# The opening of a fused attention and expert kernel: first pair head by head, its row of maxima placed by transposes, second pair's loads on ScalarE's queue

## The chip, the cores and the metric

The kernel runs on one core of a Trainium2 chip, as one launch. The metric is the device time of that launch in microseconds (us). Five engines matter here: TensorE (PE in the profile, its weight loads PEld), VectorE (DVE), ScalarE (ACT), GpSimd (POOL) and SyncE (SP), whose queue issues nearly all DMAs. Data live in SBUF (128 partitions); TensorE writes PSUM.

## The reference

Two stages, cut to what matters:

```python
# attention: q, k, v are (8, 8, 1152, 64) float32
q_pool = q.reshape(B, H, S // 2, 2, D).mean(axis=3)          # 576 queries a head
scores = scale * np.matmul(q_pool, k.transpose(0, 1, 3, 2))
scores = scores - np.max(scores, axis=-1, keepdims=True)
attn = np.exp(scores)
attn = attn / (np.sum(attn, axis=-1, keepdims=True) + 1e-09)
x = np.matmul(attn, v)                                        # then to (4608, 512)
# experts: 8 of them, one for each token
logits = x @ w_gate + modality_bias[modality_id]
e_idx = np.argmax(logits, axis=1)                             # and the gate's softmax weight
out[e_idx == e] = gate_w * (np.maximum(x[e_idx == e] @ w1[e], 0) @ w2[e])
```

All of it is computed to float32's accuracy, with float16 matmuls over high and low parts.

## The kernel before, in words

**Pairs.** The 64 heads of attention are done in 32 pairs: two heads at a time, the first on partitions 0 to 63, the second on 64 to 127. For each pair the loads bring `rawq` (queries, the two to be averaged lying in the two halves of the row), `rawk` and `rawv`. The two query halves are added (`split_q`), keys and queries are copied to float16 (`hi`, `qh`, functions `split_hi` and `split_qh`), and what the copies lose is kept as `lo` (`split_lo`).

**Maxima.** The softmax needs each query's largest score. `QB` holds the 1152 queries of a pair as nine blocks of 128. Head 0's queries stand in partitions 0 to 63 and zeros below; head 1's the other way round. Block 4 is shared: 64 queries of head 0 and 64 of head 1. So one matmul of a block with the keys `hi` of both heads gives the scores of the right head for each query. VectorE reduces them to maxima `mp`. `maxpass` does a pair; for the first pair `first_max` does blocks 0 to 4 on thirds of the keys ahead of everything, and `maxpass` the last four blocks.

**Row.** `row` takes the maxima of some blocks, turns them from a column into rows by a matmul with the identity (L792), scales them into `mr` (L801) and sends `mr` by DMA (L802) into partition 64 of `B2`.

**Scores.** `scores` makes transposed scores: a matmul with `B1` (high keys twice, over high and low queries, L888), then one with `B2` (low keys and, in partition 64, the row of the maxima, L889). So the maximum is subtracted by the matmul itself. ScalarE's exponential follows (L890, four to a third of a head's keys), then the low part `Pl` (L871 on ScalarE, L873 on VectorE). `B1` and `B2` are filled by SBUF to SBUF moves on SyncE's queue (`place_k`, `place_q`, `place_lo`, L618).

**Values.** `square` and `power` find a power of two to scale a pair's values by (L729, L735, `scales`); `values` makes their high part `VH` (L772) and low part `vl` (L765, L766), `shifted` the copy `VS` (L782). `pv` multiplies exponentials and values, three matmuls for a block (L947 to L949).

**Order.** TensorE, ScalarE, VectorE and GpSimd run in the order in which the program issues. After the opening, a loop of steps runs, 18 for a pair. In each step the letters of `ORD` say what comes when: `M` and `X` advance the maxima, `s` the scores, `v` the value products, `F` what falls due. Work is put at steps by `at`, `later` and `later_end`; the constants at the top of the file are its due steps. The value products of the first pair follow their exponentials by `LAG0` = 7 steps. `busy` issues matmuls of zeros that nothing uses.

**The opening** (L1014 to L1085) prepares pair 0 for both heads at once, then pair 1, runs `first_max` in between, places pair 0, and ends with three maxima of the rest.

After attention come routing and the experts' matmuls, which the change does not touch.

Of the kernel before, what the change touches and what calls it, by code (L numbers as in the profile page):

```python
# [22 lines left out]
P = 128  # L23
# [5 lines left out]
S = 1152  # L29
# [42 lines left out]
V0 = (0, 1, (2, 3), 3, (3, 4))  # L72
# [72 lines left out]
T_PRE = 3  # L145
# [438 lines left out]
def attention(tc, ctx, att, ident, npairs, xpool, on_two, on_split, on_scale, jobs, side, set_pm, started, ahead, hip):  # L584
# [31 lines left out]

    def move(o, i):
        nc.sync.dma_start(out=o, in_=i)  # L618

    half_q = lambda i: slice(i * 288, (i + 1) * 288)  # L620

    def load_kq(p):
        k, q = (pa.tile([P, S], F32, name="raw" + x) for x in "kq")
        st[p]["k"], st[p]["q"] = k, q
        if p == 0:
            two = lambda x: x.rearrange("p (w n) -> p w n", w=2)
            for x, i in ((q, 0), (k, 0), (k, 1), (q, 1), (k, 2)):
                if x is q:
                    nc.sync.dma_start(out=two(q)[:, :, half_q(i)], in_=two(att[p, :, S:2 * S])[:, :, half_q(i)])
                else:  # L630
                    nc.sync.dma_start(out=k[:, i * 384:(i + 1) * 384], in_=att[p, :, i * 384:(i + 1) * 384])
        else:
# [65 lines left out]
    half = [slice(0, D), slice(D, P)]  # L698

# [7 lines left out]
    def place_k(p, heads):  # L707

        s = st[p]
        for i in range(2):  # L710
            for j in heads:
                move(s["B1"][half[i], kcol(j)], s["hi"][half[j]])
# [71 lines left out]
    def row(p, mp, u0, u1):  # L784
# [13 lines left out]
        def put(pt):  # L798
# [3 lines left out]
            done = (nc.sync if p or u0 else nc.scalar).dma_start(out=B2[p % 2][D:D + 1, 2 * S + u0 * P:2 * S + u1 * P], in_=mr[0:n])  # L802
# [6 lines left out]
    def maxpass(p, mp=None):  # L809

        s = st[p]
        need(p, *(("qh", "hi0", "hi1") if p else ()))
        u0 = 0 if mp is None else 5
        two = p in TWO_ROWS
        rest = []
        if mp is None:
            mp = sm.tile([P, 9, 3], F32, name="mp")
# [20 lines left out]
    def first_max(p):  # L838

        s = st[p]  # L840
        mp = s["mp"] = sm.tile([P, 9, 3], F32, name="mp")
        for i, (u, t) in enumerate([(u, t) for us in ((0, 1), (2, 3, 4)) for t in range(3) for u in us]):
            pt = ps_sc.tile([P, 512], F32, name="psc") if i % 2 else ps_max.tile([P, 512], F32, name="pm")
            nc.tensor.matmul(pt[:, 0:384], QB[p % 2][:, u], s["hi"][:, t * 384:(t + 1) * 384], start=True, stop=True)
# [3 lines left out]
        busy(8)  # L848
        row(p, mp, 0, 5)()
# [167 lines left out]
    nc.gpsimd.memset(warm, 0.0)  # L1017
    nc.scalar.activation(warm, warm, AF.Exp)
    nc.gpsimd.memset(ones, 1.0)
    load_kq(0)  # L1020
# [9 lines left out]
    busy(7)  # L1030
    for i in range(2):
        nc.vector.memset(QB[i], 0.0)
    nc.gpsimd.memset(B2[0][D:D + 1, 0:2 * S], ROW)
    split_q(0)
    q0, qb = st[0]["q"][:, 0:SQ], QB[0].rearrange("p u n -> p (u n)")
# [583 lines left out]
```

## Time and profile before

| | |
|---|---|
| Time, median of 3 runs | 1135.43 us (1134.61 to 1135.49) |
| The profiled execution's own time | 1135.75 us |
| Its span, first to last instruction | 1134.0 us |
| TensorE busy | 1105.3 us, 97% |
| VectorE busy | 979.1 us, 86% |
| ScalarE busy | 914.1 us, 81% |
| GpSimd busy | 417.2 us, 37% |
| Granted TensorE clock, mean | 0.998 |

In the views that follow, a row of the timeline has the start, the duration, the engine, the line, the operation, what it writes and reads, its shape and count, and in brackets how long the engine was idle before and what ended that. A row of the stretches has the stretch, its length, and for PE, PEld, DVE, ACT and POOL the busy time with the count of instructions started, then the granted clock, the share of DMA and the GB/s.

### The profile page before, as it was taken

How to read it: one execution, taken by the hardware profiler on the slowest of the kernel's cores; microseconds unless marked ns; L12 is line 12 of the kernel's file. 1: busy time of each engine (PE TensorE's matmuls, PEld its weight loads, DVE VectorE, ACT ScalarE, POOL GpSimd, SP SyncE). 2: the span in 40 equal slices, each digit the busy share in tenths (PEclk: the TensorE clock that was granted, in tenths of full speed). 3: DMA queues.
4: the chain of work that ended last, by engine and by line, in shares of the span. 5: the costliest groups of instructions: out<-in, count | busy, mean ns of one | idle time of the engine just before them, and what ended most of it. 6: DMA issues, size and time to landing. Idle time of an engine off the chain costs nothing. (4 is left out here: it accounts for less than half of the span.)

```text
span 1134.0 us, 36903 instructions
## 1 busy us (share of the span) xinstructions
PE 1105.3 (97%) x15117; PEld 814.7 (72%) x15117; DVE 979.1 (86%) x1968; ACT 914.1 (81%) x1462; POOL 417.2 (37%) x408
## 2 busy tenths in 40 slices
PE   8999999999999999999999999999999999999997
PEld 4777777777777777777777777767667667667665
DVE  7999999999999999999999999887996766756754
ACT  5999999999999999999999988865556665655654
POOL 7854444354444445344444342124113112122111
PEclk9999999999999999999999999999999999999999
DMA  7677867859759768678587463499999999899993
GB/s 230 183 189 175 193 162 170 196 151 202 164 161 206 163 167 190 163 174 194 146 197 187 134 138 94 140 299 269 262 290 275 279 302 283 266 282 248 307 269 107
DMA packets 175522, 232.67 MB, mean 205 GB/s; under 512 B 92303, under 2 KB 126751, under 8 KB 175344
## 3 DMA queue, kind: packets, MB, share of 16 engines
q1 hardware_dynamic: 169254, 210.45, 71.3%
q0 software_dynamic: 6080, 19.78, 6.7%
q8 instruction: 120, 1.97, 0.7%
q14 instruction: 58, 0.48, 0.1%
q10 hardware_dynamic: 10, 0.00, 0.0%
HBM read 146.11 MB, written 18.99 MB: 146 GB/s over the span
## 5 line engine op out<-in xcount | busy, mean ns | idle before, releaser
L890 ACT ACTIVATE Pe<-psc 128x432 int32<-128x432 f32 x768 | 377.4, 526 | 44.3 <-PE psc L889 35.1
L822 DVE TENSOR_REDUCE mp<-pm 128x1 f32<-128x512 f32 x566 | 372.7, 684 | 14.2 <-PE pm L821 6.9
L947 PE MATMUL xp<-VH,Pe 128*128 128x65 f16 x2880 | 372.5, 193 | 0.0
L949 PE MATMUL xp<-VS,Pl 128*128 128x65 f16 x2880 | 371.9, 193 | 0.4 <-DVE Pl L873 0.4
L948 PE MATMUL xp<-vl,Pe 128*128 128x64 f16 x2880 | 370.6, 192 | 0.0
L948 PEld LDWEIGHTS <-Pe 128*128 128x128 f16 x2880 | 267.6, 98 | 87.5
L888 PE MATMUL psc<-B 128*128 128x432 f16 (+2 forms) x1152 | 304.0, 286 | 2.4 <-ACT Pe L890 2.2
L889 PE MATMUL psc<-B 65*128 65x432 f16 (+2 forms) x1152 | 304.7, 287 | 0.2 <-DMA B<-mr 0.2
L947 PEld LDWEIGHTS <-Pe 128*128 128x128 f16 x2880 | 272.0, 98 | 45.6 <-issue 7.5
L949 PEld LDWEIGHTS <-Pl 128*128 128x128 f16 x2880 | 266.5, 97 | 0.7 <-DVE Pl L873 0.5
L871 ACT ACTIVATE Pl<-Pe 128x1152 f16<-128x1152 uint16 (+1 forms) x190 | 219.3, 1154 | 6.0
L821 PE MATMUL pm<-hi,QB 128*128 128x512 f16 x566 | 213.8, 379 | 8.4 <-DVE mp L822 8.0
L683 POOL TENSOR_TENSOR lo<-rawk,hi 128x576 f16<-128x576 f32 (+1 forms) x68 | 87.9, 1296 | 196.5 <-ACT hi L667 183.6
L770 POOL TENSOR_SCALAR VH<-rawv,sc 128x512 f16<-128x512 f32 (+1 forms) x60 | 103.3, 1732 | 153.5 <-PE xp L949 73.8
L1296 PE MATMUL ph<-xpart,w1l 128*128 128x256 f16 x544 | 148.3, 273 | 0.0
L1295 PE MATMUL ph<-xpart,w1h 128*128 128x256 f16 x544 | 148.3, 273 | 0.0
L1294 PE MATMUL ph<-xpart,w1h 128*128 128x256 f16 x544 | 148.3, 273 | 0.0
L889 PEld LDWEIGHTS <-B 65*128 65x128 f16 x1152 | 112.8, 98 | 25.9 <-issue 3.2
L888 PEld LDWEIGHTS <-B 128*128 128x128 f16 x1152 | 112.5, 98 | 9.2 <-issue 3.8
L1300 DVE SCALAR_TENSOR_TENSOR hl<-ph,hh 128x512 f16<-128x512 f32 x72 | 49.7, 690 | 77.6 <-ACT hh L1299 77.5
L1299 ACT ACTIVATE hh<-ph 128x512 f16<-128x512 f32 x72 | 43.0, 598 | 87.5 <-PE ph L1296 87.5
L1389 PE MATMUL po<-w2h,hl 128*128 128x512 f16 x288 | 109.1, 379 | 0.0
(276 smaller groups left out, 1924.4 us busy)
## 6 DMA issues: line engine op xcount, KB each, us to landing
w2r<-in_w_dram SPq DMA_DIRECT2D x76, 512.0 KB
w1r<-in_w_dram SPq DMA_DIRECT2D x72, 512.0 KB
rawv<-in_att_dram SPq DMA_DIRECT2D x32, 576.0 KB
B<-hi SPq DMA_DIRECT2D x128, 144.0 KB
rawq<-in_att_dram SPq DMA_DIRECT2D x31, 576.0 KB
rawk<-in_att_dram SPq DMA_DIRECT2D x31, 576.0 KB
B<-qh SPq DMA_DIRECT2D x128, 72.0 KB
B<-lo SPq DMA_DIRECT2D x64, 144.0 KB
```

Source lines behind the costliest of these rows:

```text
L821: nc.tensor.matmul(pm, QB[p % 2][:, u], s["hi"][:, t * 512:(t + 1) * 512], start=True, stop=True)
L822: nc.vector.tensor_reduce(mp[:, u, t:t + 1], pm, op=ALU.max, axis=AX.X)
L871: nc.scalar.activation(low, rest, AF.Copy, scale=LOW)
L888: nc.tensor.matmul(o, b1[:, ks], b1[:, qs], start=True, stop=False, skip_group_check=True)
L889: nc.tensor.matmul(o, b2[:, ks], b2[:, qs], start=False, stop=True, skip_group_check=True)
L890: nc.scalar.activation(Pe[:, D + x0:D + x1], pt, AF.Exp, scale=1.0 / 16)
L947: nc.tensor.matmul(out, Ph[:, qs], vh[:, c, j, 0:D + 1], start=c == 0 and g == 0, stop=False, skip_group_check=True)
L948: nc.tensor.matmul(out[:, 0:D], Ph[:, qs], vl[:, c, j], start=False, stop=False, skip_group_check=True)
L949: nc.tensor.matmul(out, Pl[:, qs], vs[:, c, j, 0:D + 1], start=False, stop=c == NKC - 1, skip_group_check=True)
L1294: nc.tensor.matmul(o, hi[:, c, fs], xh[:, :, c], start=c == 0, stop=False)
L1295: nc.tensor.matmul(o, hi[:, c, fs], xl[:, :, c], start=False, stop=False)
L1296: nc.tensor.matmul(o, lo[:, c, fs], xh[:, :, c], start=False, stop=c == 3)
```

## The change

The first pair's preparation is done one head after the other. Head 0's keys are copied into a tile `hz` of their own, with zeros in partitions 64 to 127; head 1's keys stay in `hi`, with zeros in partitions 0 to 63. Blocks 0 to 3 of the first maxima use `hz` alone, and block 4 is two matmuls added up, one over each tile. Loads, adds, copies, remainders and moves of the first pair are split by head.

The row of the first five blocks no longer goes through `mr` and a DMA. The maxima are reduced into the last column of `spread`, a tile of zeros 65 wide for each block, and five transposes bring that column to partition 64 of PSUM, from where VectorE (two blocks) and ScalarE (three) write it to `B2`.

The second pair's queries and keys are loaded from ScalarE's queue. Its copies (`split_q`, `split_hi`, `split_qh`) come after the row and its remainders (`split_lo`) at step 3. The first pair's square and scale are done in the opening, its values two steps earlier. Small memsets move from GpSimd to VectorE and ahead of the first add. The numbers of filler matmuls change, and two loads are issued behind a move.

```diff
+T_L1 = 3
-V0 = (0, 1, (2, 3), 3, (3, 4))
+V0 = (None, None, (0, 1), 2, (2, 5))
-T_PRE = 3
+T_PRE = 2
...
-        B2.append(const.tile([D + 1, 2 * KQ], F16, name=f"B2_{i}"))
+        B2.append(const.tile([D + 1, 2 * KQ + (0 if i else D)], F16, name=f"B2_{i}"))
...
     def move(o, i):
-        nc.sync.dma_start(out=o, in_=i)
+        moved[:] = [nc.sync.dma_start(out=o, in_=i).ins]
+    def behind(ins, fn):
+        with tc.issue_after(ins):
+            fn()
...
         if p == 0:
-            for x, i in ((q, 0), (k, 0), (k, 1), (q, 1), (k, 2)):
...
+            for i in range(2):
+                nc.scalar.dma_start(out=two(q[half[0]])[:, :, half_q(i)], in_=two(att[p, half[0], S:2 * S])[:, :, half_q(i)])
+            for i in range(3):
+                nc.sync.dma_start(out=k[half[0], third(i)], in_=att[p, half[0], third(i)])
+            nc.sync.dma_start(out=q[half[1]], in_=att[p, half[1], S:2 * S])
+            nc.sync.dma_start(out=k[half[1]], in_=att[p, half[1], 0:S])
+        elif p > 1:
...
+    def first_max(mp):
+        for i, (u, t) in enumerate([(u, t) for us in ((0, 1), (2, 3), (4,)) for t in range(3) for u in us]):
...
+            keys = (hz, st[0]["hi"])[0:1 + u // 4]
+            for h in keys:
+                nc.tensor.matmul(pt[:, 0:384], QB[0][:, u], h[:, third(t)], start=h is hz, stop=h is keys[-1])
             nc.vector.tensor_reduce(mp[:, u, t:t + 1], pt[:, 0:384], op=ALU.max, axis=AX.X)
             busy(1, 256)
             yield
-        busy(8)
-        row(p, mp, 0, 5)()
+    def first_row(mp, spread):
+        nc.vector.tensor_reduce(spread[:, :, D], mp[:, 0:5], op=ALU.max, axis=AX.X, negate=True)
+        ends(0)
+        for us in ((0, 1), (2, 3, 4)):
+            pt = some(0)
+            for i, u in enumerate(us):
+                nc.tensor.transpose(pt[0:D + 1, i * P:(i + 1) * P], spread[:, u], ident)
+            x0, x1 = us[0] * P, (us[-1] + 1) * P
+            o, x = B2[0][D:D + 1, 2 * S + x0:2 * S + x1], pt[D:D + 1, 0:x1 - x0]
+            if us[0]:
+                nc.scalar.activation(o, x, AF.Copy, scale=1.0 / ROW, bias=16.0 * math.log(PSC) / ROW)
+            else:
+                nc.vector.tensor_scalar(o, x, 1.0 / ROW, 16.0 * math.log(PSC) / ROW, op0=ALU.mult, op1=ALU.add)
+        made.add((0, "row5"))
...
-    busy(7)
+    busy(9)
...
+    spread = const.tile([P, 5, D + 1], F32, name="turned")
+    nc.gpsimd.memset(spread, 0.0)
+    hz = pa.tile([P, S], F16, name="hi")
     split_q(0)
+    for j in range(2):
+        nc.vector.memset((hz, st[0]["hi"])[j][half[1 - j]], 0.0)
+    for b in B2:
+        nc.gpsimd.memset(b[D:D + 1, 0:2 * S], ROW)
+    for i in range(3):
+        nc.vector.memset(VH[i][:, :, :, D:D + 2], 1.0)
+        nc.vector.memset(VS[i][:, :, :, D:D + 2], 2.0 ** -16)
+    for pe, pl in PT:
+        for x in (slice(0, D), slice(D + W3, 2 * D + W3)):
+            nc.vector.memset(pe[:, x].bitcast(F32), 0.0)
+            nc.vector.memset(pl[:, x], 0.0)
+    add = lambda eng, r, c: eng.tensor_tensor(q0[r, c], q0[r, c], q1[r, c], op=ALU.add)
+    add(nc.vector, half[0], half_q(0))
+    add(nc.gpsimd, half[0], half_q(1))
...
+    for i in range(3):
+        nc.scalar.copy(hz[half[0], third(i)], k0[half[0], third(i)])
+        if i < 2:
+            if npairs > 1:
+                nc.scalar.dma_start(out=st[1]["qk"[i]], in_=att[1, :, slice((1 - i) * S, (2 - i) * S)])
+            nc.scalar.copy(qb[half[0], half_q(i)], q0[half[0], half_q(i)])
         for _ in range(2):
             next(first)
...
+    few, rest = slice(0, 5 * P - SQ), slice(5 * P - SQ, SQ)
+    add(nc.vector, half[1], few)
+    for j, h in enumerate((hz, hi)):
+        if j:
+            add(nc.gpsimd, half[1], rest)
+            nc.scalar.copy(hi[half[1]], k0[half[1]])
+            nc.scalar.copy(qb[half[1], SQ:5 * P], q0[half[1], few])
+            square(0)
+            nc.scalar.copy(qb[half[1], 5 * P:S], q0[half[1], rest])
+        nc.scalar.copy(qh[half[j]], q0[half[j], every])
+        nc.gpsimd.tensor_tensor(lo[half[j], 0:S], k0[half[j]], h[half[j]], op=ALU.subtract)
+        nc.gpsimd.tensor_tensor(lo[half[j], S:KQ], q0[half[j], every], qh[half[j]], op=ALU.subtract)
+        place_k(0, (j,))
+        place_q(0, (j,))
+        place_lo(0, (j,), 1)
+        place_lo(0, (j,), 0)
+    drain(first)
+    power(0)
+    busy(4)
+    first_row(mp0, spread)
     if npairs > 1:
         split_q(1)
         for i in range(3):
             split_hi(1, i)
         split_qh(1)
-        for i in (3, 4, 5, 6, 0, 1, 2):
-            split_lo(1, i)
-    drain(first)
...
-    mxq.append(maxpass(0, mp0))
+    mxq.append(second_max(mp0))
     for _ in range(T_PRE):
-        busy(2)
+        busy(1)
         advance(mxq, 1)
-    busy(2)
-    at(T_RT, 0, started)
+    at(T_RT, 0, lambda ins=moved[0]: behind(ins, started))
...
+            for i in (3, 4, 5, 6, 0, 1, 2):
+                go(T_L1 - b, split_lo, i)
             go(T_P1 - b, place, end=False)
             go(T_M1 - b, lambda p: mxq.append(maxpass(p)), end=False)
-            go(T_LV, load_v)
+            go(T_LV, lambda p, ins=moved[0]: behind(ins, lambda: load_v(p)))
```

More of the change, by code (lines that the diff above doesn't have):

```diff
@@ L615, in need @@
         assert all((p, n) in made for n in names), f"pair {p}: {names} are not made yet"
+    moved = []
     def move(o, i):
-        nc.sync.dma_start(out=o, in_=i)
+        moved[:] = [nc.sync.dma_start(out=o, in_=i).ins]
+    def behind(ins, fn):
+        with tc.issue_after(ins):
+            fn()
     half_q = lambda i: slice(i * 288, (i + 1) * 288)
+    third = lambda i: slice(i * 384, (i + 1) * 384)
+    half = [slice(0, D), slice(D, P)]
     def load_kq(p):
@@ L711, in place_k @@
             for j in heads:
-                move(s["B1"][half[i], kcol(j)], s["hi"][half[j]])
+                move(s["B1"][half[i], kcol(j)], (s["hi"] if p or j else hz)[half[j]])
     def place_lo(p, heads, k):
@@ L847, in first_max, with second_max @@
             yield
-        busy(8)
-        row(p, mp, 0, 5)()
+    def first_row(mp, spread):
[12 more added lines that the diff above has]
+        made.add((0, "row5"))
+    def second_max(mp):
+        s = st[0]
+        for u in range(5, 9):
+            for t in range(2):
+                pm = ps_max.tile([P, 512], F32, name="pm")
+                nc.tensor.matmul(pm, QB[0][:, u], s["hi"][:, t * 512:(t + 1) * 512], start=True, stop=True)
+                nc.vector.tensor_reduce(mp[:, u, t:t + 1], pm, op=ALU.max, axis=AX.X)
+                yield
+        pm = ps_max.tile([P, 512], F32, name="pm").rearrange("p (n k) -> p n k", k=P)
+        for i in range(4):
+            nc.tensor.matmul(pm[:, i], QB[0][:, 5 + i], s["hi"][:, 1024:S], start=True, stop=True, skip_group_check=True)
+        nc.vector.tensor_reduce(mp[:, 5:9, 2], pm, op=ALU.max, axis=AX.X)
+        yield
+        later_end(FIN if now[0] > NSTEP else 1, row(0, mp, 5, 9))
     def scores(p, j, r):
@@ new lines, in attention @@
+    qb = QB[0].rearrange("p u n -> p (u n)")
+    q0, q1 = (st[0]["q"][:, i * SQ:(i + 1) * SQ] for i in range(2))
+    k0, hi, qh, lo = (st[0][x] for x in ("k", "hi", "qh", "lo"))
+    for b in B2:
[7 more added lines that the diff above has]
+            nc.vector.memset(pl[:, x], 0.0)
@@ L1036, in attention @@
+    first = first_max(mp0)
+    add = lambda eng, r, c: eng.tensor_tensor(q0[r, c], q0[r, c], q1[r, c], op=ALU.add)
+    every = slice(0, SQ)
+    add(nc.vector, half[0], half_q(0))
+    add(nc.gpsimd, half[0], half_q(1))
     if npairs > 1:
         load_kq(1)
-    first = first_max(0)
-    for n, i in ((0, 0), (2, 1), (2, 2)):
+    for i in range(3):
+        nc.scalar.copy(hz[half[0], third(i)], k0[half[0], third(i)])
         if i < 2:
-            both = st[0]["q"].rearrange("p (w n) -> p w n", w=2)
-            nc.vector.tensor_tensor(both[:, 0, half_q(i)], both[:, 0, half_q(i)], both[:, 1, half_q(i)], op=ALU.add)
-        if i == 0:
-            nc.scalar.copy(qb[0:D, half_q(0)], q0[0:D, half_q(0)])
-        split_hi(0, i)
-        if i == 1:
-            nc.scalar.copy(qb[0:D, half_q(1)], q0[0:D, half_q(1)])
+            if npairs > 1:
+                nc.scalar.dma_start(out=st[1]["qk"[i]], in_=att[1, :, slice((1 - i) * S, (2 - i) * S)])
+            nc.scalar.copy(qb[half[0], half_q(i)], q0[half[0], half_q(i)])
@@ L1108, in attention @@
             go = lambda t, f, *a, p=p: at(t, p, lambda: f(p, *a))
-        go(sq, square)
-        go(power_, power)
+        if p:
+            go(sq, square)
+            go(power_, power)
         for i, t in enumerate(vh):
```

49 lines of the change are left out of this document (8 added, 41 removed).

## The prediction

> **What bounds the kernel now.** I read the page's busy shares first, then the busy time by stretches of ten microseconds, then the opening engine by engine in order of time, because everything the change touches runs before the third pair.
>
> ```profile
> span 1134.0 us, 36903 instructions
> PE 1105.3 (97%) x15117; PEld 814.7 (72%) x15117; DVE 979.1 (86%) x1968; ACT 914.1 (81%) x1462; POOL 417.2 (37%) x408
> ...
> 10.00:20.00 10.00, 10.00 (x48) 5.31 (x47) 8.60 (x17) 2.57 (x7) 9.58 (x35) 1.00 0.82 196
> 20.00:30.00 10.00, 7.61 (x49) 3.99 (x48) 8.28 (x21) 9.90 (x17) 7.06 (x5) 1.00 0.64 220
> 30.00:40.00 10.00, 9.89 (x160) 7.34 (x160) 9.60 (x23) 9.91 (x18) 6.68 (x6) 1.00 0.96 276
> ...
> 19.40:30.20 10.80, 8.41 (x55) 4.51 (x54) 9.08 (x22) 10.64 (x18) 7.80 (x9) 1.00 0.63 211
> 30.20:49.20 19.00, 18.45 (x304) 13.98 (x303) 18.46 (x45) 18.76 (x33) 14.70 (x12) 1.00 0.70 188
> ```
>
> TensorE is busy 97% of the span and from 30 us on it hardly pauses, so the time is its remaining work plus the moment when that work can run without gaps. That moment is the first value product. From 19.4 to 30.2 us it is ScalarE that has no idle time (10.64 of 10.80), while TensorE starts only 55 instructions; from 30.2 on both are full. What the change can win is therefore the shift of the first value product, and it is worth as much at the end. The rows of the opening, ScalarE, VectorE, GpSimd, TensorE and SyncE's queue in turn:
>
> ```profile
> 4.26 0.43 ACT L1044 CAST QB<-rawq 64x288 f16<-64x288 f32 x1 [1.96 <-DVE rawq L1042]
> 4.60 0.51 ACT L667 CAST hi<-rawk 128x384 f16<-128x384 f32 x1
> 13.00 1.34 ACT L667 CAST hi<-rawk 128x384 f16<-128x384 f32 x3 [2.87 <-DMA rawk<-in_att_dram]
> 14.24 0.67 ACT L657 CAST qh<-rawq 128x576 f16<-128x576 f32 x1
> 16.76 1.28 ACTq L802 DMA_DIRECT2D B<-mr  x1
> 19.40 1.12 ACT L890 ACTIVATE Pe<-psc 128x432 int32<-128x432 f32 x2 [4.50 <-PE psc L889]
> 20.42 1.16 ACT L729 ACTIVATE vl<-rawv 128x1152 f16<-128x1152 f32 x1
> 21.57 0.52 ACT L890 ACTIVATE Pe<-psc 128x432 int32<-128x432 f32 x1
> ...
> 1.26 1.14 DVE L1032 MEMSET QB<- 128x576 uint32 x2
> 3.77 0.46 DVE L1042 TENSOR_TENSOR rawq<-rawq 128x288 f32<-128x288 f32 x1 [1.36 <-DMA rawq<-in_att_dram]
> 5.67 0.56 DVE L845 TENSOR_REDUCE mp<-pm 128x1 f32<-128x384 f32 x1 [1.45 <-PE pm L844]
> 9.42 0.56 DVE L845 TENSOR_REDUCE mp<-pm 128x1 f32<-128x384 f32 x1 [0.51 <-PE pm L844]
> 14.70 0.55 DVE L845 TENSOR_REDUCE mp<-pm 128x1 f32<-128x384 f32 x1
> 15.28 0.17 DVE L788 TENSOR_REDUCE m<-mp 128x5 f32<-128x15 f32 x1
> 16.45 0.28 DVE L801 TENSOR_SCALAR mr<-pj 5x128 f16<-5x128 f32 x1 [0.99 <-PE pj L792]
> 23.02 0.22 DVE L743 TENSOR_SCALAR sc<-half 128x1 int32<-128x1 int32 x2
> 23.15 0.14 DVE L743 TENSOR_SCALAR scales<-half 128x1 int32<-128x1 int32 x1
> ...
> 1.13 2.01 POOL L1033 MEMSET B<- 1x2304 f16 x1
> 11.82 1.40 POOL L648 TENSOR_TENSOR rawq<-rawq 128x576 f32<-128x576 f32 x1
> 13.59 2.79 POOL L683 TENSOR_TENSOR lo<-rawk,hi 128x288 f16<-128x288 f32 x4 [0.37 <-ACT hi L667]
> 16.34 1.55 POOL L683 TENSOR_TENSOR lo<-rawq,qh 128x192 f16<-128x192 f32 x3
> 17.84 0.13 POOL L1073 MEMSET VH<- 128x36 f16 x1
> 19.72 2.01 POOL L1079 MEMSET B<- 1x2304 f16 x1
> 32.82 1.29 POOL L683 TENSOR_TENSOR lo<-rawq,qh 128x576 f16<-128x576 f32 x1
> ...
> 16.14 0.27 PE L792 MATMUL pj<-ident,m 128*5 128x128 f32 x1
> 19.02 0.35 PE L889 MATMUL psc<-B 65*128 65x432 f16 x1
> 30.22 0.19 PE L947 MATMUL xp<-VH,Pe 128*128 128x65 f16 x1
> ...
> 3.76 0.43 SPq L633 DMA_DIRECT2D rawq<-in_att_dram  x1
> 4.24 0.65 SPq L634 DMA_DIRECT2D rawk<-in_att_dram  x1
> ```
>
> The last maximum ends at 15.25; its row is turned by TensorE at 16.14, scaled by VectorE at 16.45, issued as a DMA at 16.76 and used at 19.02; the first exponential starts at 19.40. Note where pair 1's copies on ScalarE stand: at 13.00 and 14.24, in the 4.50 us hole ahead of 19.40. And note the square of the values (L729): it stands behind the second exponential, and the third one starts 1.15 us after it (20.42 to 21.57).
>
> **The change, part by part.** ScalarE, VectorE and GpSimd run their instructions in the order of the program, so I lay out the new order with the durations above.
>
> *VectorE's start.* The two memsets of QB (1.14 together, from 1.26) are followed by two more of the same size (the empty halves of the two keys' copies), to 3.54, and then by 22 small ones moved from GpSimd (VH, VS and the edges of Pe and Pl). No small memset of VectorE is in the trace. Bounds: on GpSimd the 22 took 17.84 to 19.72, 1.88 us; at the 0.11 us that two tiny operations take in the row at 23.02 they would take 2.4, at the whole 0.14 of the row at 23.15 they take 3.1; free they cannot be, and at half of GpSimd's price they are 0.9. I take GpSimd's, the same shapes. The first add then starts at 5.42, not 3.77; by then the data are there, since even the 128-partition load landed at 3.77.
>
> *ScalarE's start.* Two loads are issued ahead of the table load; then third by third: the key's copy, a load of pair 1, the query block's copy. With the add's end at 5.88: query block 0.34 (4.26 to the next start at 4.60), key third 0.51, issue of pair 1's second load, query block 0.34, last key third 0.51. An issue of such a load takes 0.43 or 0.65 on SyncE's queue; the only issue on ScalarE took 1.28, for another shape. I take 0.65, the same load, with 0.43 and 1.28 as ends. The last third of head 0's keys is copied at 8.3.
>
> *GpSimd.* Today one subtraction serves both heads; now each head has its own, at the same length along the row, and a 1-partition memset (2.01 for 2304 elements) shows that fewer partitions do not make GpSimd quicker. So from 8.3: head 0's key remainder 2.75 (13.59 to 16.34), query remainder 1.25 to 1.29, the add of the other query half 1.24 (512/576 of 1.40), head 1's key remainder 2.75, query remainder 1.25, then pair 1's add 1.40: it ends at 18.9. Both memsets of B (2.01 each) lie ahead, from 1.4 to 5.5, beside VectorE's, and cost nothing as long as the chain starts at 8.3. Pair 1's remainders (seven operations, 2.79 + 1.55) go to the end of step 3.
>
> *The row.* Maxima: the first reduce comes about 1.1 us behind the query block's copy as today (4.26 to 5.67 is 1.41 with the key's copy between), so at 7.0, and since all data are there, 15 run at the 0.53 of today (9.42 to 14.70 in ten): last one to 15.0, or 15.6 if the three double matmuls of the shared block each cost TensorE another 0.2. That is today's 15.25; the halves' earlier landing is eaten by the memsets. From there: reduce 0.17, five transposes at 0.27, ScalarE's copy of 384 numbers at about the 0.51 of a 384-wide cast: in place at some 17.5. The DMA's 2.3 us (16.76 to 19.02) is gone.
>
> *What stands between row and scores.* Behind its copy of the row ScalarE now has pair 1's three key copies (1.34) and its query copy (0.67), and the first exponential is queued behind them. That query copy waits for GpSimd's add of pair 1 at 18.9; ScalarE itself is there at 18.8. Either way the first exponential starts at about 19.6, against 19.40: **0.2 later**, although the row is 1.5 earlier. Ends: 18.6 if the maxima end 0.7 sooner, 21 with the dear ends of the memsets and the issue.
>
> *Behind the first exponential.* The square and its 1.15 us leave the stretch in which ScalarE is the bound; they now run in a hole near 12 us, where ScalarE waits for GpSimd. The values' copies (L772, L782) move by two steps but all stay ahead of the eighth exponential. So the first value product comes 1.15 - 0.2 = 0.9 earlier, about 29.3. GpSimd's remainder of the values' second part ends near 33.5 instead of 32.1, since pair 1's remainders are ahead of it; it is needed by the 26th product of L948:
>
> ```profile
> 30.20:36.80 6.60, 3.43 (x25) 2.31 (x25) 1.00 0.97 265
> ```
>
> The 25 before it last to 36.8, so it has over 2 us left; without that cover every microsecond would count. The rest is hidden: T_PRE, the fillers, the memset of the transposes' source (GpSimd waits later anyway), B2's padding, the scale's five tiny operations on VectorE (today at 22.84, then beside the transposes), the place moves of head 0 (their last source is ready at 12.3, the row at 17.5) and of head 1 (18 us, needed after step 9), pair 1's values and the router's setup issued behind a move.
>
> **Sum.** First exponential +0.2, square -1.15: -0.9 us. The profiled execution's own time is 1135.75 (span 1134.0 and 1.75 around it), which gives 1134.85; it stands 0.32 above the median of the three runs shown, so on their scale **1134.5**.
>
> **Rivals.** *Scores begin with the row* (what the change says): if pair 1's copies do not hold the first exponential back, it starts at 17.9, 1.5 earlier, and with the square the gain is 2.65: 1132.8. For it: the row's DMA was the last wait at 19.02. Against it: copies and exponentials share one engine in program order. Chance 0.25.
>
> *Each small memset costs its full duration.* Then VectorE is 1.2 us later (3.1 for 1.88), GpSimd's chain with it, the first exponential is at 20.8 and the sum is +0.3: 1135.7. Against it: the tiny operations at 23.02 and 23.15 start 0.13 apart or less though each lasts 0.14. Chance 0.12. By the Trainium skill, "VectorE: DVE Perf Modes", The DRAIN you can't avoid, a VectorE operation does not start until the pipe of the one before is empty, which speaks for this rival; the overlapping rows at 23.02 and 23.15 speak against that reading, and no row before the change has small memsets.
>
> *Issuing loads holds ScalarE* (the slower side): at 1.28 for each of its four issues ScalarE reaches its first key copy at 4.8, the second query block at 9.1 and the last key third at 9.6 instead of 8.3. Everything behind shifts by 1.35, the first exponential to 20.95, and the sum is +0.4: 1135.8. It decides from about 1.1 us an issue. For it: the one row of a ScalarE issue. Against: that one has 5 partitions. Chance 0.10; with the memsets' dear price on top it ends near 1136.5.
>
> *The square's room is not used*: if VectorE's maxima, 9.08 of 10.80 busy in that stretch, set the first value product, only the 0.2 remains: 1135.6. Against: VectorE has 1.7 us idle there. Chance 0.13.
>
> **How the numbers follow.** Forecast 0.40. Without the far cases its own range is 1133.8 to 1135.2. For 8 in 10 the range must reach the first rival below and the slower ones above: 1132.2 to 1136.4. A measurement of this kernel tells 0.2%, 2.3 us, from no change. Faster by that: most of the first rival and a little of the forecast, 0.28. Slower by that: both dear prices together with a stall that I don't see, 0.07. Within it: 0.65.
>
> **What will show it.** Right: VectorE's first add near 5.4; the row written without a DMA near 17.5; on ScalarE three key copies and a query copy behind it, the last one waiting for GpSimd's add; the first exponential at 19 to 20; no square behind it; the first value product near 29.3; TensorE full from there. Wrong: an exponential before 18.5, a first add past 6.5, issues over 1 us on ScalarE, or a gap of TensorE at pair 1's or pair 2's maxima because the moves behind GpSimd's later remainders land late.

## The result: slower, and where the time goes in the profile after

The changed kernel takes 1140.86 us (median of 6 runs) beside 1135.02 for the kernel before on the same chip: 1.0052 of it, with an interval of 1.0041 to 1.0064. It is slower by 5.8 us, outside the predicted range of 1132.2 to 1136.4. The page of the changed kernel, its span and busy shares:

```profile
span 1139.2 us, 36916 instructions
PE 1104.9 (97%) x15116; PEld 813.8 (71%) x15116; DVE 980.7 (86%) x1992; ACT 916.5 (80%) x1466; POOL 424.3 (37%) x386
```

TensorE is as busy as before (1104.9 against 1105.3), so the 5.2 us by which the span grew are idle time of TensorE. The busy time by stretches gives a first idea of where. Columns: stretch, its length, then busy time of PE, PEld, DVE, ACT and POOL with instruction counts, the granted clock, the DMA share and GB/s. First the changed kernel, then the kernel before in the one of these stretches that the prediction does not show (each sum is over 0 to 80 us):

```profile
10.00:20.00 10.00, 6.16 (x23) 3.29 (x24) 5.84 (x18) 4.87 (x9) 7.41 (x5) 0.66 0.84 233
...
30.00:40.00 10.00, 8.80 (x124) 6.10 (x122) 9.89 (x24) 8.38 (x15) 8.34 (x8) 1.00 0.78 205
...
60.00:70.00 10.00, 7.30 (x129) 5.66 (x127) 7.28 (x17) 7.25 (x12) 7.84 (x16) 1.00 0.56 145
...
sum 80.00, PE 67.13 PEld 45.17 DVE 66.97 ACT 61.10 POOL 58.50; mean PE 8.39 PEld 5.65 DVE 8.37 ACT 7.64 POOL 7.31
```

```profile
60.00:70.00 10.00, 8.80 (x140) 6.56 (x139) 9.43 (x19) 8.94 (x15) 5.90 (x7) 1.00 0.62 165
...
sum 80.00, PE 72.56 PEld 49.01 DVE 69.50 ACT 62.63 POOL 57.02; mean PE 9.07 PEld 6.13 DVE 8.69 ACT 7.83 POOL 7.13
```

TensorE is busy 67.13 us of the first 80, against 72.56: 3.8 us less from 10 to 20 us, 1.1 from 30 to 40, 1.5 from 60 to 70. The first of these stretches says little by itself, because fillers count as busy: they take 7.72 us of it in the kernel before and 4.12 in the changed one, and there the granted clock is 0.66. The first exponential of each pair (the 1st, 25th, 49th and 73rd of its line) is the better measure. It stands 1.88 us late at pair 0, 2.71 at pair 1, 4.56 at pair 2, and 4.6 from pair 3 to pair 12 (5.3 from pair 24 on), so nearly all of the loss is there at pair 3:

| first exponential, us | pair 0 | pair 1 | pair 2 | pair 3 |
|---|---|---|---|---|
| before | 19.40 | 45.25 | 70.26 | 92.29 |
| after | 21.29 | 47.96 | 74.82 | 96.89 |

**The first loss.** The opening in the timeline of the changed kernel (start, duration, engine, line, names; in brackets the idle time before and what ended it):

```profile
4.93 0.41 DVE L1090 TENSOR_TENSOR rawq<-rawq 64x288 f32<-64x288 f32 x1
5.39 0.33 ACTq L1100 DMA_DIRECT2D rawk<-in_att_dram  x1
6.97 0.51 ACT L1097 CAST hi<-rawk 64x384 f16<-64x384 f32 x1
11.07 1.15 ACT L1111 CAST hi<-rawk 64x1152 f16<-64x1152 f32 x1 [3.02 <-DMA rawk<-in_att_dram]
12.42 0.50 PE L851 MATMUL pm<-hi,QB 128*128 128x384 f16 x2 [2.56 <-ACT QB L1112]
14.25 0.56 DVE L852 TENSOR_REDUCE mp<-pm 128x1 f32<-128x384 f32 x1 [0.27 <-PE pm L851]
14.54 1.16 ACT L737 ACTIVATE vl<-rawv 128x1152 f16<-128x1152 f32 x1 [2.17 <-DMA rawv<-in_att_dram]
15.85 0.16 PE L743 MATMUL pm<-ss,ones 128*128 128x1 bf16 x1 [1.42 <-ACT vl L737]
15.87 1.87 PE L1065 MATMUL pj<-zero 128*128 128x512 f16 x4
17.54 1.27 PE L863 MATMUL pm<-ident,turned 128*65 128x128 f32 x5
18.84 0.48 ACT L867 ACTIVATE B<-pm 1x384 f16<-1x384 f32 x1 [1.84 <-PE pm L863]
19.35 1.34 ACT L677 CAST hi<-rawk 128x384 f16<-128x384 f32 x3
20.60 0.67 ACT L667 CAST qh<-rawq 128x576 f16<-128x576 f32 x1
21.29 0.95 ACT L927 ACTIVATE Pe<-psc 128x432 int32<-128x432 f32 x2
```

Until 6.97 all is ahead of the prediction. Then ScalarE waits 3.02 us for head 1's keys and 2.17 for the values. The square (L737) reads those values, and TensorE has its matmul of the scale (L743) and four fillers written ahead of the five transposes. The maxima are done at 14.81, in the predicted time, but the transposes start at 17.54. Pair 1's copies follow the row at 19.35, and the first exponential follows them.

**The second loss.** TensorE's largest pause is ahead of pair 3's first maximum. Its row and SyncE's queue ahead of it; the longest wait of that queue in the list of waits (us in all, times, longest); and then the queue of the kernel before at the same place:

```profile
69.20 0.39 PE L828 MATMUL pm<-hi,QB 128*128 128x512 f16 x1 [1.97 <-DMA QB<-qh]
...
62.30 0.40 SPq L217 DMA_DIRECT2D xs<-z  x1
62.74 1.26 SPq L644 DMA_DIRECT2D rawk<-in_att_dram  x1
64.10 1.11 SPq L621 DMA_DIRECT2D QB<-qh  x2
65.25 0.58 SPq L648 DMA_DIRECT2D rawv<-in_att_dram  x1
...
67.66 0.81 SPq L810 DMA_DIRECT2D B<-mr  x1
```

```profile
SPq L217 <- POOL z L216: 7.9, 1, 7.9
```

```profile
51.52 1.83 SPq L633 DMA_DIRECT2D rawq<-in_att_dram  x1
53.39 0.43 SPq L634 DMA_DIRECT2D rawk<-in_att_dram  x1
53.93 0.37 SPq L638 DMA_DIRECT2D rawv<-in_att_dram  x1
60.10 0.38 SPq L216 DMA_DIRECT2D xs<-z  x1
60.59 1.20 SPq L618 DMA_DIRECT2D QB<-qh  x2
```

Counted in the queue's order, these loads of 576 KB each are pair 4's queries (rawq) and keys (rawk) and pair 3's values (rawv). Before, they left by 53.93, ahead of the zero store that waits for GpSimd's setup. After, pair 4's keys and pair 3's values stand behind that store. The keys, which nothing reads before 84.68, stand directly ahead of pair 3's query-block moves; the values stand ahead of pair 2's row (mr), with two moves and pair 5's queries between.

### The profile page after: what moved, and what is told of

The parts are those of the page before. It is cut to its first block, busy times and chain, and to the rows that moved or that the text cites. A ratio compares the mean times of both kernels' runs of the same rounds, so it can differ in the third digit from the quotient of the medians.

```text
span 1139.2 us, 36916 instructions
## 1 busy us (share of the span) xinstructions
PE 1104.9 (97%) x15116; PEld 813.8 (71%) x15116; DVE 980.7 (86%) x1992; ACT 916.5 (80%) x1466; POOL 424.3 (37%) x386
## 3 DMA queue, kind: packets, MB, share of 16 engines
q10 hardware_dynamic: 576, 1.47, 0.4%
## 5 line engine op out<-in xcount | busy, mean ns | idle before, releaser
L829 DVE TENSOR_REDUCE mp<-pm 128x1 f32<-128x512 f32 x558 | 368.3, 684 | 16.7 <-PE pm L828 9.1
L926 PE MATMUL psc<-B 65*128 65x432 f16 (+2 forms) x1152 | 304.9, 287 | 0.5 <-DMA B<-mr 0.4
L828 PE MATMUL pm<-hi,QB 128*128 128x512 f16 x558 | 211.3, 379 | 11.0 <-DVE mp L829 8.9
L693 POOL TENSOR_TENSOR lo<-rawk,hi 128x576 f16<-128x576 f32 (+1 forms) x64 | 85.2, 1334 | 192.5 <-ACT hi L677 187.2
L926 PEld LDWEIGHTS <-B 65*128 65x128 f16 x1152 | 112.8, 98 | 26.0 <-issue 2.6
L1440 PE MATMUL po<-w2h,hh 128*128 128x512 f16 x288 | 109.3, 379 | 0.0
```

What stands on the lines that cost most here:

```text
L828: nc.tensor.matmul(pm, QB[p % 2][:, u], s["hi"][:, t * 512:(t + 1) * 512], start=True, stop=True)
L829: nc.vector.tensor_reduce(mp[:, u, t:t + 1], pm, op=ALU.max, axis=AX.X)
L926: nc.tensor.matmul(o, b2[:, ks], b2[:, qs], start=False, stop=True, skip_group_check=True)
```

## The experiments

All were timed beside the kernel before; a ratio is to it, with its interval. "The mended kernel" is the changed one with pair 1's loads back on SyncE's queue and the setup issued when its step comes.

**The place of pair 1's loads.**

```diff
-        elif p > 1:
+        else:
             nc.sync.dma_start(out=q, in_=att[p, :, S:2 * S])
...
-            if npairs > 1:
-                nc.scalar.dma_start(out=st[1]["qk"[i]], in_=att[1, :, slice((1 - i) * S, (2 - i) * S)])
```

> The changed kernel with pair 1's queries and keys loaded from SyncE's queue again, behind pair 0's values; nothing else differs. Theory A (two queues of loads side by side delay pair 0): head 1's keys, on which ScalarE waited until 11.07 us, are there before 9.5, the values, on which it waited until 14.54, before 12; the first exponential moves from 21.29 to about 19.6, the first value product from 32.7 to about 30.8, and the time falls by 1.5 to 2.5 us from the changed kernel's 1140.9. Rival B (loads of 64 partitions are slow by themselves): head 1's keys still land past 10.5 and the values past 13.5, and the time changes by less than 0.7 us.

Measured 1138.70 us, 1.0036 (1.0022 to 1.0050). ScalarE in this run (two lines fewer, so L1109 is L1111 above):

```profile
8.95 1.15 ACT L1109 CAST hi<-rawk 64x1152 f16<-64x1152 f32 x1 [0.89 <-DMA rawk<-in_att_dram]
10.37 1.16 ACT L737 ACTIVATE vl<-rawv 128x1152 f16<-128x1152 f32 x1
15.52 0.48 ACT L867 ACTIVATE B<-pm 1x384 f16<-1x384 f32 x1 [1.80 <-PE pm L863]
16.03 1.34 ACT L677 CAST hi<-rawk 128x384 f16<-128x384 f32 x3
17.59 0.67 ACT L667 CAST qh<-rawq 128x576 f16<-128x576 f32 x1 [0.22 <-POOL rawq L658]
18.28 0.95 ACT L927 ACTIVATE Pe<-psc 128x432 int32<-128x432 f32 x2
```

The keys come 2.1 us earlier, the square waits for nothing, and the first exponential is 3.0 us earlier than in the changed kernel and 1.1 earlier than before. So the place of these two loads is the first loss; the run puts them on another queue and behind pair 0's values at once, and does not separate the two. Pair 1 is 0.3 ahead of the kernel before, but pair 3 is 3.5 behind: the second loss is still there, and larger (3.8 us between pairs 1 and 3, 1.9 in the changed kernel).

**The square at its old place.** The other way to take it out from ahead of the row:

```diff
-V0 = (None, None, (0, 1), 2, (2, 5))
+V0 = (0, 1, (2, 3), 3, (3, 4))
...
-            square(0)
...
-    power(0)
     busy(4)
```

> The changed kernel with the square and the scale of pair 0's values back in the steps where they were before, and the values' copies at their old steps. Theory A (the square waits for late values and holds back ScalarE's next copies, GpSimd's last remainder and TensorE's transposes): the row is in place near 17 instead of 19.3, the first exponential comes at about 19.2 instead of 21.29, but the square's 1.15 us return to the stretch behind it: first value product about 31.3 instead of 32.7, time 1.0 to 1.6 us lower. Rival (GpSimd's chain alone holds the first exponential): first exponential within 0.5 us of 21.3, and the time 1 us higher.

Measured 1142.57 us, 1.0084 (1.0056 to 1.0113). The first exponential is at 18.30, with the keys as late as in the changed kernel: without the square ahead of the row it comes 3 us earlier. Part of that may be TensorE's clock, which stays at 1.00 here until 41.9 and is 0.50 from 13 to 20 us in the changed kernel. But TensorE then pauses at 39.26, until pair 2's query-block moves have landed:

```profile
42.76 0.61 PE L828 MATMUL pm<-hi,QB 128*128 128x512 f16 x1 [3.50 <-DMA QB<-qh]
```

The gain was lost, and more, in SyncE's queue: those moves stand at 37.63 behind two loads of 576 KB (36.44 and 37.07). From 41.91 to 48.74 the granted clock is 0.50, and pair 3 is 5.9 us late: pause and clock together, not the queue alone.

**The zero store off SyncE's queue.**

```diff
-        nc.sync.dma_start(out=self.xs[T - NT * P:T, DM:XW].rearrange("(t p) d -> p t d", p=P), in_=z)
+        nc.gpsimd.dma_start(out=self.xs[T - NT * P:T, DM:XW].rearrange("(t p) d -> p t d", p=P), in_=z)
```

> The changed kernel with one DMA moved: the router's store of zeros is issued by GpSimd instead of SyncE. Theory C (on SyncE's queue that store waits 7.9 us, until 62.3, for a memset of GpSimd; pair 4's keys stand behind it, and pair 3's query moves behind those, so TensorE idles 1.97 us at 67.2): the gap is gone, pair 2's second half and everything behind it come 1.8 us earlier, time 1139.0. Rival (pair 3's queries are late on GpSimd anyway): the gap stays within 0.4 us, time 1140.9.

Measured 1139.26 us, 1.0044 (1.0030 to 1.0058), with pair 3 still 4.36 late. The pause ahead of L828 is gone, another of 1.56 us stands ahead of pair 2's last scores (L926). Pair 3's moves now wait 10.0 us for GpSimd's copy (L665), and the store, now issued by GpSimd, stands ahead of that copy; what this costs is measured below. So the store was not the cause but the place where the cause showed, and that the time came near the 1139.0 expected is luck.

**The row alone.** The kernel before, with its first half row put in place by transposes and nothing else of the change:

```diff
-        busy(8)
-        row(p, mp, 0, 5)()
+        busy(4)
+        first_row(mp)
```

> The kernel before with one part of the change: the first row is put in place by five transposes instead of a DMA; pair 1's copies stay ahead of it. If the row is what the scores wait for, the first exponential moves from 19.40 to about 17.7, the first value product from 30.2 to about 28.7, and the time falls by about 1.5 us to 1133.5. Rival (ScalarE, VectorE and TensorE are full behind it, so an earlier start is lost again by 50 us): the first exponential is as early, but pair 1 starts within 0.5 us of 45.25 and the time stays at 1135.0.

Measured 1134.92 us, 1.0004 (0.9993 to 1.0014). The row is done at 16.50 (ScalarE's copy starts at 16.02), yet the first exponential comes at 18.97, only 0.43 earlier. TensorE's first matmul of the scores:

```profile
18.41 0.35 PE L903 MATMUL psc<-B 128*128 128x432 f16 x1
```

In program order TensorE has fillers and the next maxima ahead of it, and it ran them without a pause up to it. In the kernel before it is the same: TensorE has no idle time ahead of its matmuls at 18.84 and 19.02, so the row's DMA held nothing up, and the 0.43 may be no more than the four fillers that this edit also leaves out. But the 0.43 is kept: every pair up to pair 21 starts 0.37 to 0.43 earlier than before, so here an earlier start is not lost again by 50 us. The interval of the time is too wide to show 0.4 us.

**The setup when its step comes.** The first experiment's kernel, with the setup no longer tied to a place move; then the same with the zero store on GpSimd's queue; and that with pair 1's loads left on ScalarE's queue.

```diff
-    at(T_RT, 0, lambda ins=moved[0]: behind(ins, started))
+    at(T_RT, 0, started)
```

> The run before with pair 1's loads back on SyncE's queue, and the router's setup no longer held behind a place move (it is issued when its step comes). In the static order of SyncE's queue pair 3's keys then stand ahead of pair 2's place moves again, as before the change; the zero store still stands ahead of pair 3's query-block moves, and pair 3's values and pair 4's queries still stand directly ahead of pair 2's row. Theory O (what was lost after pair 1 is the order of SyncE's queue): first exponential 18.3, pair 1's 44.95, the 2.15 us gap of TensorE before the maxima of L828 gone, the 1.83 us gap ahead of L926 still there: pair 2 at 70.3 to 71.0, pair 3 at 93.5 to 94.3, time 1136.5 to 1137.2. Rival P (the work itself is denser around pair 1, whatever the queue's order): pair 3 stays at 95.8, time 1138.7.

> As the setup run, and the zero store leaves SyncE's queue for GpSimd's: in the static order pair 3's values now stand ahead of its query-block moves and nothing that waits for GpSimd stands between. Theory O: neither gap, pairs 1 to 3 at 44.9, 70.0, 92.0, time 1134.0 to 1134.8, as before or up to 0.5 us less. Rival P: pair 3 at 95 or later, time 1138.

> The changed kernel with pair 1's loads left on ScalarE's queue, and the other two things mended (setup when its step comes, zero store on GpSimd's queue). Theory O with the late loads as the separate first loss: first exponential 20 to 21.3, pair 1 at +2.7 on before (47.9), and no more after it: pair 3 at 94.9, time 1137.4. Rival P: +4.6 at pair 3 as in the changed kernel, time 1139.3 to 1140.9. Rival Q (the loads' place is all of it, the order costs nothing): as the changed kernel, 1140.9.

The first of them measured 1134.92 us, 1.0002 (0.9993 to 1.0012). One line of issue order gives back 3.8 us (3.97 to 0.18 beside the kernel before), and with the two loads (5.84 to 3.97, 1.9 us) the loss of 5.8 is gone. The setup's own loads now leave SyncE's queue at 5.57, not at 42.78, and that moves what is written behind them: pair 4's keys (the ones that the expectation calls pair 3's) are issued at 40.50, and the pauses at pair 3's maxima and pair 2's row are gone but for 0.57 us. I had expected the second to stay: the time came out 1.6 lower than forecast.

The store on GpSimd's queue makes it worse: 1137.06, 1.0023 (1.0012 to 1.0034). GpSimd without and with it:

```profile
59.23 0.11 POOL L216 MEMSET z<- 128x18 f32 x1
59.29 0.66 POOL L665 CAST qh<-rawq 128x576 f16<-128x576 f32 x1
```

```profile
59.55 0.11 POOL L216 MEMSET z<- 128x18 f32 x1
59.97 1.27 POOL L217 DMA_DIRECT2D xs<-z  x1 [0.31 <-POOL z L216]
61.24 0.69 POOL L665 CAST qh<-rawq 128x576 f16<-128x576 f32 x1
```

Issuing one small store costs GpSimd 1.6 us, and pair 3's copy, its moves and pair 2's row are all later by 1.9 to 2.0. My expectation had the queue's order right and forgot the engine that issues. The third run, 1138.21 and 1.0035 (1.0022 to 1.0049), differs from the second only in the two loads: +1.15 us, with the first exponential 1.8 later (20.42 against 18.61) and pair 3 1.74 later. The intervals of the two times overlap.

**Pair 1's copy behind the first exponentials.**

```diff
         for i in range(3):
             split_hi(1, i)
-        split_qh(1)
+        at(1, 1, lambda: split_qh(1))
```

> As the queue-order run, and pair 1's copy of the queries (L667, 0.67 us on ScalarE, which stood between the first scores' matmuls, done at 17.33, and the first exponential at 18.28) moved behind the first three exponentials. Theory S (ScalarE's copies hold the first exponential): it starts at 17.4, 0.9 us earlier than in the queue-order run, and pairs 1 to 3 come 0.5 to 0.9 earlier; time 1133.2 to 1134.0. Rival T (ScalarE has the same work to do before pair 1's first exponential either way): first exponential 17.4, but pair 1 within 0.2 us of the queue-order run, and the time too. Rival U: pair 1's query-block moves, now issued some 3 us later and behind two loads, make pair 1's maxima late, and it is slower by 1 us or more.

Measured 1140.08 us, 1.0043 (1.0029 to 1.0057): the slow rival was right. The first exponential moves to 17.61, 1.0 earlier, so ScalarE's copies do hold it. But pair 1's query-block moves leave at 21.81, behind two loads, instead of 19.38 without this edit, and TensorE waits for them. Here too the granted clock then is 0.50 for 6.8 us (25.91 to 32.74), which is part of the loss:

```profile
26.86 1.46 PE L828 MATMUL pm<-hi,QB 128*128 128x512 f16 x3 [1.99 <-DMA QB<-qh]
```

**Who takes back the start's gain.** With both causes undone the first exponential is 1.0 us earlier than before and the time the same. Two suspects were tried on that kernel, alone and together: the second half of the row by four transposes, and the router's setup 12 steps later. The fourth run is the second with pair 1's loads on ScalarE's queue.

```diff
-        later_end(FIN if now[0] > NSTEP else 1, row(0, mp, 5, 9))
+        later_end(FIN if now[0] > NSTEP else 1, second_row(mp))
...
-T_RT = 24
+T_RT = 36
```

> The setup run (pair 1's loads on SyncE's queue, setup when its step comes), and the second half of pair 0's row (query blocks 5 to 8) is put in place by four transposes and a copy of 1x512 on VectorE, not by a transpose, a copy and a DMA. In the setup run TensorE idles 0.93 us (23.28 to 24.21) ahead of L925 until that DMA has landed, and has idled 4.4 us between 18 and 46 us against 2.5 in the kernel before. Theory M (this idle time is what takes back the 1 us won at the first exponential): the gap goes, the row is there at about 23.1, pair 1's first exponential at 44.2 to 44.7 in place of 45.15, pair 3 at 91.3 to 92.0 in place of 92.30, time 1134.0 to 1134.6. Rival N (ScalarE's or VectorE's work up to pair 1 is what counts): pair 1 at 45.0 to 45.4, pair 3 at 92.2 to 92.5, time 1134.9.

> The setup run with the router's setup 12 steps later (T_RT 36 for 24): in the static order of GpSimd's queue it stands behind pair 3's copy and remainders, and the zero store behind pair 2's row on SyncE's queue. Theory G (GpSimd's 7.2 us of setup, 52.10 to 59.29, ahead of pair 3's copy of the queries L665, takes back the gain): the copy at 52, pair 3 0.3 to 0.6 earlier than 92.30, time 1134.4. Rival M (TensorE's own idle time takes it back): pair 3 within 0.2 of 92.30, time 1134.9.

> The two edits together: second half of the row by transposes, setup 12 steps later. If each works on a wait of its own, the gains add: pair 3 at 91.0 to 91.7, time 1133.5 to 1134.3. Rival: the later of the two waits decides and the other edit adds nothing: as the better of the two alone.

> As the setup-later run, but pair 1's loads stay on ScalarE's queue as the change has them: it differs from that run in nothing but the place of those two loads, with no store on GpSimd's queue. Theory A (they make the head's keys and the values late): first exponential 20 to 21.3 against 18.4, pair 1 at 46.8 to 47.9, and later pairs keep 1.5 to 2.7: time 1136.6 to 1137.6. Rival: the loss at the start is absorbed by slack further on, pair 3 within 0.5 of the setup-later run, time 1135.3 or less.

Measured: 1134.59, ratio 1.0000 (0.9991 to 1.0010); 1137.74, 1.0023 (1.0009 to 1.0037); 1135.83, 1.0018 (1.0005 to 1.0032); 1139.77, 1.0053 (1.0036 to 1.0070). The row by transposes removes the pause that it was aimed at, and pair 3 stays at 92.38, as rival N had it (pair 1, at 45.60, is later than either theory); a place move that landed late had held the first exponential at 18.81. The later setup brings pair 2 to 68.97, 1.3 us before the kernel before, as pair 3's moves now leave at 52.72. Then the store waits 5.3 us for its memset, until 70.94, in front of pair 3's place moves, and pair 3's row comes late:

```profile
92.80 0.34 PE L926 MATMUL psc<-B 65*128 65x432 f16 x1 [2.96 <-DMA B<-mr]
```

So the wait moved by one pair, and behind it the clock falls: it is 0.50 from 93.37 to 96.78, and pair 4 is 3.51 late. This is one execution, of 1139.27, of a kernel whose times lie between 1134.44 and 1139.80. Together the two edits have the same pause (2.73 us) and the same fall of the clock. The fourth run is 2.0 us slower than the second in the median, but the traces do not show why: in the two profiled executions it is the faster one (1137.14 against 1139.27), with no fall of the clock at pair 3.

**The store at the head of the setup**, with the setup 12 steps later: on the mended kernel, on the kernel before, and on the mended kernel with pair 1's loads on ScalarE's queue.

```diff
         nc, con = self.nc, self.con
+        z = con.tile([P, NT, 2], F32, name="z")
+        nc.gpsimd.memset(z, 0.0)
+        nc.sync.dma_start(out=self.xs[T - NT * P:T, DM:XW].rearrange("(t p) d -> p t d", p=P), in_=z)
         wg = con.tile([P, 4, E], F32, name="wg")
```

> The setup-later run, with the zero store and the memset it waits for at the head of the router's setup, not at its end. In the setup-later run pair 2's first exponential came 1.29 us earlier than in the kernel before (pair 3's query-block moves no longer waited for GpSimd), and then the store, which waited until 70.94 for its memset, held pair 3's place moves (71.43 to 78.68) and pair 3's row came 3 us late. Theory G2 (that wait is all of the 3.5 us): no gap of TensorE at 89.84, pairs 3 and later 0.8 to 1.3 earlier than before (91.0 to 91.5 at pair 3), time 1133.2 to 1133.9. Rival H (GpSimd's work itself, whose add of pair 4 came at 70.88 for 64.59, or TensorE's total work decides): pair 3 at 92.3 or later, time 1134.9 or more.

> The kernel before, with the setup 12 steps later and the zero store at its head, and nothing of the change. Theory G2: here too pair 2 comes earlier, by what the setup alone gives (0.3 to 0.8 us), and the time falls by as much, to 1133.8 to 1134.1; then what the changed start adds is the difference to the run above. Rival M: the kernel before has no such wait (its place moves and its row stood in another order), nothing within 0.2 us, 1134.5.

> As the store-first run, but pair 1's loads stay on ScalarE's queue as the change has them: it differs from that run in those two loads alone. Theory A: first exponential 1.0 to 2.0 later than there, pair 1 1.1 to 2.7 later, and pairs 3 and on keep 1 to 2.5 of it: time 1135 to 1136.5. Rival: the loss is absorbed, pair 3 within 0.5 of the store-first run, time within 0.6 of it.

Measured: 1135.78, 1.0011 (1.0001 to 1.0021); 1135.92, 1.0004 (0.9993 to 1.0015); 1136.83, 1.0021 (1.0012 to 1.0030). The store's wait is gone and pair 4 is 1.8 us earlier than without this edit (there the clock had fallen, here it does not), yet neither kernel gains on the one before; the first has a pause of 1.35 us at 40.65, where pair 2's query-block moves land late, that the mended kernel does not have. In the kernel before pair 2 moves 1.47 us forward and pair 3 only 0.24. My theory that the setup takes the gain back falls. With the two loads the median is 1.05 us higher, but the intervals overlap, and of the profiled executions the one with the loads on ScalarE's queue is the faster (1136.09 against 1136.66): its first exponential is 0.85 later, its pair 1 is 0.27 earlier and its pair 3 0.81.

## Why the prediction was wrong, step by step

**Held.** VectorE's first add came at 4.93, not 5.42: the 22 memsets took 1.15 us (3.78 to 4.93), each lasting 0.09 to 0.11 and starting 0.04 to 0.07 after the one before, below GpSimd's price, and that rival falls. Of ScalarE's four issues the first two took 1.52 us together, a little above the forecast of 0.65 each; pair 1's two took 0.38 and 0.33 and held nothing up: the query copy at 5.38 and the key copy behind it start 0.34 apart, as in the kernel before (4.26 and 4.60), with an issue beside them. That rival falls too. The last key third was copied by 7.48 (forecast 8.3), the maxima ended at 14.81 (15.0 to 15.6). The mechanism "pair 1's copies stand between row and scores" is right and was shown: with the loads put back the copies run at 16.03 and 17.59, the exponential starts at 18.28, and taking one copy away brings it to 17.6. Its size was off: with the data there the first exponential comes 1.1 earlier than before (18.28 for 19.40), not 0.2 later.

**Misread.** Pair 1's copies, at 13.00 and 14.24, do not lie in ScalarE's idle 4.50 us ahead of 19.40; by the prediction's own rows they end at 14.91, where it begins. And the row's DMA, whose 2.3 us the prediction strikes out and which stood as "the last wait at 19.02" for the first rival, held nothing up: TensorE was at work up to that matmul.

**Failed: "a hole near 12 us" for the square.** The prediction took the data as there. The values landed at 14.5, and by program order the scale's matmul stands ahead of the transposes, so the row waited for the values: +1.9 us instead of +0.2 at the first exponential, and 32.72 instead of 29.3 at the first value product. In four other runs with the same opening and the same two loads (zero store; setup and store; setup later; store first) the first exponential comes at 20.00, 20.42, 19.45 and 19.30, so the profiled execution of the changed kernel is the latest of five; the last section says what the clock adds. The transfers were never summed. In the stretch from 3 to 11 us, the changed kernel and then the run with the loads on SyncE's queue (queue, packets, MB, share of 16 engines):

```profile
q1 hardware_dynamic: 404, 1.18, 61.4%
q10 hardware_dynamic: 352, 0.83, 39.9%
```

```profile
q1 hardware_dynamic: 625, 2.06, 89.2%
q10 hardware_dynamic: 218, 0.22, 10.9%
```

ScalarE's queue is q10. It also carries head 0's queries, which are all of its 10.9% in the second run, so pair 1's loads, first read at 18.49, took some 29% of the engines' time (39.9 less 10.9, an estimate) while pair 0's keys and values were waited for. Three pairs of runs that differ in these two loads alone give 1.05, 1.15 and 2.0 us, the first experiment 1.9. All four medians point the same way, but in every pair the two intervals overlap, and in the pairs of 1.05 and 2.0 the profiled executions go the other way: the loads cost something like 1 to 2 us, and how much is not settled. The Trainium skill, "DMA: Bandwidth & Descriptors", Issuing engines are not separate DMA queues, says that transfers started by different engines run on the same 16 DMA engines and interleave, and that a second issuer saves only issue time; the two rows agree, and this rule belonged into the prediction as a rival.

**Failed: "hidden" for the setup issued behind a move.** It was put at nothing without a reason. What it moves is the order of SyncE's queue: 576 KB of keys directly ahead of pair 3's query-block moves, and pair 2's row later behind them. With the keys out of the way both pauses go but for 0.57 us, although pair 3's values still stand ahead of the row (61.81 and 64.69). That is 3.8 us in the order in which the two causes were undone; in the changed kernel's own trace it is the 1.9 us between pairs 1 and 3. The prediction named a gap of TensorE at pair 1's or pair 2's maxima as what would prove it wrong, but put it down to GpSimd's remainders and gave it no price.

**Failed: "square -1.15" and "worth as much at the end".** The mended kernel has its first exponential 1.02 earlier, its first value product at 29.55, 0.67 earlier, pair 1 0.10 earlier and pair 3 at 92.30, where it was before. The sum counted on 1.15 us less between first exponential and first value product once the square has left that stretch; it is 11.17 us here and 11.43 in the changed kernel, against 10.82 before. The mended kernel's stretches, and two rows of its timeline:

```profile
20.00:30.00 10.00, 6.81 (x52) 3.62 (x49) 8.06 (x15) 8.57 (x15) 9.77 (x11) 1.00 0.75 228
30.00:40.00 10.00, 9.24 (x150) 6.90 (x149) 9.60 (x22) 9.52 (x17) 6.89 (x6) 1.00 0.96 268
```

```profile
28.14 0.38 PE L828 MATMUL pm<-hi,QB 128*128 128x512 f16 x1 [0.22 <-DVE mp L829]
...
28.92 0.53 ACT L927 ACTIVATE Pe<-psc 128x432 int32<-128x432 f32 x1 [1.26 <-PE psc L926]
```

ScalarE, no longer the bound, idles 1.26 us for scores, which TensorE has behind maxima that wait for VectorE: from 20 to 40 us TensorE is busy 16.05 us here and 17.50 in the kernel before. This is the rival "the square's room is not used", with its VectorE, which had 0.13. What brings pair 3 to 92.0 to 92.4 in four kernels whose first exponentials lie between 18.4 and 19.4 is not settled: the row, GpSimd's setup and the store were tried, and none of them is it alone. Nor is an earlier start always lost: the kernel before with the row alone kept its 0.43 and has pair 3 at 91.87. Another 0.7 us of the changed kernel's loss appears only between pairs 12 and 24. Beside the kernel before, the traces of the other runs have steps of -0.4 to +1.2 us there too, so it need not come from the change.

## What to carry to other kernels

Sum the bytes against the landing times when a load is moved or added: a transfer that nobody waits for yet still takes its share from those that somebody does. When an edit shifts when something is issued, write out the new order of every queue that it passes, pairs ahead, and look for large loads that nobody needs yet in front of small moves that an engine waits for. And before a microsecond at the start is counted at the end, find out which engine is next behind the one that is relieved.

## What the runs showed of the hardware that was not expected

Two load queues side by side moved less in all, not only less each: from 7 to 11 us the 16 DMA engines are busy throughout in both runs, but the changed kernel moves 267 GB/s and the first experiment, with one queue, 335. It is 229 to 295 in the six runs with the loads on two queues and 330 to 349 in the eight with one. What is in flight differs too (head 1's keys, a load of 64 partitions, land later with two queues), so whether the second queue or this mix lowers the rate is not shown. Two stretches of the changed kernel, and a row of the last run of all (store first, loads on ScalarE's queue):

```profile
7.00:11.00 4.00, 2.70 (x19) 1.59 (x17) 3.94 (x9) 1.05 (x3) 3.44 (x2) 1.00 1.01 267
15.00:19.00 4.00, 3.15 (x11) 1.81 (x11) 1.00 (x7) 2.14 (x5) 1.78 (x2) 0.50 0.64 141
...
12.72 0.50 PE L851 MATMUL pm<-hi,QB 128*128 128x384 f16 x2 [2.83 <-ACT QB L1112]
```

The second row shows a second price of the wait. In the changed kernel TensorE has 2.56 us without a matmul, then little work, and its granted clock is 0.50 from 13.22 to 20.05. The four fillers and five transposes take 1.87 and 1.27 us for 1.02 and 0.73 in the first experiment. The run with the zero store on GpSimd's queue has the same opening at the full clock. There the row's copy starts 2.94 us after the square (13.92 to 16.86), against 4.30 (14.54 to 18.84), but the first exponential follows the square by 6.08 us against 6.75, because GpSimd's add for pair 1 is then what it waits for. So of the 1.88 us some 0.7 are the clock and the rest is not, an estimate from these two executions.

The length of the gap alone does not decide whether the clock falls: it fell during or soon after gaps of 2.44, 2.56 and 2.58 us, and did not with 2.47 or, in the third row, 2.83. In all the traces the changes of the clock lie whole multiples of 3.41 us apart, so the stretches to look at are the 3.41 us between such points. In the stretch before the fall TensorE was busy 0.86 us in the changed kernel, and 1.08 and 1.36 in the two others at this place; in the run of the third row the emptiest such stretch (10.81 to 14.23) has 1.48, and the clock stays. Later in the traces the clock also fell after a stretch with 1.85, so no sharp limit is shown. The Trainium skill, "TensorE: Matmul & The Clock Gate", Why this matters for your kernels, asks for no idle gaps beyond some 3 us; here gaps of 2.44 to 2.58 us, with few matmuls around them, were enough in three executions.
